# Sigmoid attention with a ReGLU layer behind it on one core: four more slices of the hidden layer as a unit of seven products, and helper work put elsewhere

## The chip, the core and the metric

The kernel runs on one core of a Trainium2 chip, with all its engines: TensorE (PE in the profile, its weight loads PEld), VectorE (DVE), ScalarE (ACT), GpSimd (POOL), SyncE (SP) and the DMA engines. The metric is the device time of one execution in microseconds (us). Three runs of the kernel before took 388.02, 388.04 and 389.07 us; their median, 388.04, is the number that the change is measured against.

## The reference, cut to what matters

```python
# q, k, v: [8 batches, 12 heads, 448 tokens, 64], fp32
scores = q @ k.T / 8 - log(448)
x = (sigmoid(scores) @ v)          # heads side by side: [3584 tokens, 768]
out = (relu(x @ w_gate) * (x @ w_val)) @ w_out   # 768 -> 1536 -> 768
```

The attention has no softmax: each score goes through a sigmoid by itself. The layer behind it multiplies a gated half with a value half.

## The kernel before, in words

**Units.** A batch has three groups g of four heads, and each group seven chunks of 64 keys. One pair (g, c) is a *qk unit* (`qk_unit`, L299): PE makes the scores of four heads in two PSUM banks, and ACT puts each bank through the sigmoid (L187) into an SBUF tile PT. When all seven chunks of a group are there, `pv_group` (L307, matmuls at L257) multiplies them with v into two banks, and DVE copies these, scaled, into the transposed x (`xT`, L184). The hidden layer is cut into twelve slices f of 128 columns. For one batch and one slice, `gv` (L311) makes a gate bank and a value bank (L322), takes the relu of the gate on ACT (L334) or on DVE (L336), and multiplies the two on DVE into `hT` (L343).

**Seven products.** Where two batches or two halves of a batch are there together, the kernel uses Strassen's scheme: a 2x2 block product with seven products instead of eight, at the price of sums of blocks on DVE before it (S from the weights, T or X from the data) and of additions behind it. `gv_split` (L698) does four slices f for the two halves of one batch, `gv_pair` (L598) two slices for two batches, `down_pair` (L452) the last product for two tiles of 128 tokens. A unit of `gv_split` is called s0 or s4 here, by its first slice; one of `down_pair` y(g, p), with g the pair of batches and p the pair of tiles. The sums over `w_out` are T1 to T4 (`weight_sums`, L399); the sums of slices for s0 and s4 are made step by step in batch 1 (`early_sum_steps`, L560).

**PSUM.** There are eight banks in a ring. `bank` (L77) gives the next one, and `later` (L85) moves banks to the ring's end. A matmul that starts in a bank waits until whoever read its last content is done; PE runs its matmuls in the order of the program, so all that follows waits too.

**The order of the work** is written out by hand (`manual_schedule`): each engine runs its instructions in the order in which the program calls them. The 21 qk units of batch b are cut into *bursts* (`cuts`, L936 and L938). Behind each burst PE does one piece of the hidden layer for batches that are already through, and while that runs, ACT works off the burst's sigmoids. In batch 1 the pieces are a queue of half units (batch 0's 256 and 192 tokens one after the other, `push_first`, L770, `ffn_mix`, L774), so many after each burst as `mix` says (L948), with PE transposes of batch 1's keys and queries hung in between (`hooks`). In batch 2 they are `work`: u8, s0, u9, s4, u10, u11 (L888), where u8 is a plain `gv` of batch 1 with slice 8. In batch 3 they are y(0,0), y(0,1) and y(0,2) for the first two batches. A `down_pair` may have a further burst in its middle (`amid`); those in `SUMS_LATE` (L407) make the next unit's sums around it.

**Keys and queries** from batch 2 on are transposed by DMA: `dma_transposes` (L218) copies ("re-lays") a group's k and q into a tile `rel`, of which there are two, and SP sends a transposing DMA into `qkT`. Loads from HBM go through POOL's queue, in order; `hold` (L866) is a tiny POOL copy that reads a `qkT` tile, so that the loads behind it start only when that transpose has landed. In the kernel before, `late_loads` (L873) in the last stretch of batch 1 puts batch 2's v, batch 3's k and q and `w_out` behind such a hold.

Of the kernel before, what the change touches and what calls it, by code (L numbers as in the profile page):

```python
# [18 lines left out]
def kernel(  # L19
# [38 lines left out]
    ysbp = ctx.enter_context(tc.tile_pool(name="ysbp", bufs=4))  # L58
    gsbp = ctx.enter_context(tc.tile_pool(name="gsbp", bufs=6))
    first_sbuf = ExitStack()  # L60
    early = first_sbuf.enter_context(tc.tile_pool(name="early", bufs=1))
# [33 lines left out]
    def tiles_of(b):  # L95
        if b not in in_tiles:
            pool = early if b == 1 else inp
# [58 lines left out]
    load(1, 1, 2, "kq")  # L156
    load_gv(6, 9)
    load_v(1)
    load(1, 2, 3, "kq")
    load_gv(9, 12)  # L160

# [55 lines left out]

    def dma_transposes(b, g):  # L218
        k16, q16, _ = in_tiles[b]
        rel = relp.tile([P, TW, P], FP16, tag="rel", name="rel")  # L220
        for ti, t16 in enumerate((k16, q16)):
            nc.vector.tensor_copy(  # L222
                rel[:, ti * NCH : (ti + 1) * NCH, :].rearrange("p c (h d) -> p h c d", h=2),
                t16[:, 2 * g : 2 * g + 2, :].rearrange("p h (c d) -> p h c d", c=NCH),
            )
        nc.sync.dma_start_transpose(
            qkT_of(b, g)[:], rel[:].rearrange("p c x -> p (c x)")
        )

    def row_of(r, hh):  # L230
# [139 lines left out]
    def open_late():  # L370
        first_sbuf.close()
        pool = ctx.enter_context(tc.tile_pool(name="late", bufs=1))
        T = pool.tile([P, 3, HF, HM], FP16, tag="T", name="T")
        late["T"] = [T[:, 0], T[:, 1], wo[:, 0:HF, HM:DM], T[:, 2]]
        late["odd"] = pool.tile([P, NFC, P], FP16, tag="odd", name="odd")
        late["X"] = pool.tile([P, 3, HD, S], FP16, tag="X", name="X")
        late["sums"] = ctx.enter_context(tc.tile_pool(name="sums", bufs=2))

    def sub(o, a, b):
# [26 lines left out]
    FRESH = {1: 0, 2: 0, 3: NPP}  # L406
    SUMS_LATE = {(1, 0), (1, 1), (2, 0), (2, 1), (3, NPP)}  # L407
    odd = {}
# [43 lines left out]
    def down_pair(g, p, beside, then, last, first_copy, amid=None):  # L452
# [106 lines left out]

    def early_sum_steps(j, f):  # L560
        views = []
        for i in range(3 * j, 3 * j + 3):
            t = early.tile([P, 2, 512], FP16, tag=f"PT{i}", name="S")
            flat = t[:].rearrange("p a y -> p (a y)")[:, 0 : HD * 2 * P]
            views.append(flat.rearrange("p (x y) -> p x y", y=2 * P))
        yield lambda: gate_sums(f, f + 2)
        yield from unit_sum_steps(("s", f), f, views)

    def unit_sum_steps(key, f, tiles):
# [3 lines left out]
        S3, A22 = wv[:, 0:HD, fs], wv[:, HD:NDC, fs]  # L573
        sums[key] = S1, S2, S4
        return (
# [5 lines left out]
    def batch_blocks(g, ks):  # L581
        x1, x2 = xT_tiles[2 * g], xT_tiles[2 * g + 1]
        lo, hi = slice(*ks), slice(HD + ks[0], HD + ks[1])
        return [late["X"][:, i, lo] for i in range(3)] + [x1[:, lo], x1[:, hi], x2[:, lo], x2[:, hi]]

# [12 lines left out]
    def gv_pair(g, f, beside, first_copy):  # L598
        x1, x2 = xT_tiles[2 * g], xT_tiles[2 * g + 1]
        T1, T2, T4 = (late["X"][:, i] for i in range(3))  # L600
        B11, B21, T3, B22 = x1[:, 0:HD], x1[:, HD:NDC], x2[:, 0:HD], x2[:, HD:NDC]
# [82 lines left out]
    def split_sums(b):  # L684
        tile_ = xTp.tile([P, NPAIR, S], FP16, tag="xT", name="X2")
        flat = tile_[:].rearrange("p a s -> p (a s)")
# [5 lines left out]
        B11, B21, B12, B22 = x[:, 0:HD, 0:SQ], x[:, HD:NDC, 0:SQ], x[:, 0:HD, SQ:S], x[:, HD:NDC, SQ:S]  # L692
        sub(T1, B12, B11)
        sub(T2, B22, T1)
        sub(T4, B21, T2)
        sub(T3, B22, B12)

    def gv_split(b, f, beside):  # L698
# [8 lines left out]
        for j in range(4):  # L707
            us, fs = slice(j % 2 * P, (j % 2 + 1) * P), slice((f + j) * P, (f + j + 1) * P)
            S1, S2, S4 = (t[:, :, us] for t in sums[("s", f + j // 2 * 2)])
            sets.append((  # L710
                wg[:, 0:HD, fs], wg[:, HD:NDC, fs], wv[:, HD:NDC, fs],
                S1, S2, wv[:, 0:HD, fs], S4,
            ))
# [136 lines left out]
    slots[5].pv()  # L850
    push_first(1, range(0, 4))
    for f0 in range(4, 12, 2):
        for half in range(2):
            for f in range(f0, f0 + 2):
                push_first(half, (f,), (half, f) not in ((0, 9), (1, 8)))

# [8 lines left out]

    def hold(b, g):  # L866
        nc.gpsimd.tensor_copy(gate[0:1, :], qkT_tiles[(b, g)][0:1, 0, 0:2])
# [12 lines left out]

    work = deque()

    pending = []

    def push_group(g):
# [22 lines left out]
    def next_work(jobs=(), alone=False, amid=None, ahead=()):  # L908
# [11 lines left out]
        if kind == "y":  # L920
            down_pair(g, i, beside, prepare, not work, scaled_act if alone else scaled, amid)
        elif amid:
# [11 lines left out]
    for b in range(1, B):  # L934
        if b == 1:
            cuts, pv_at = (0, 3, 6, 9, 13, 17, 21), {3: (0, 2), 5: (1, 2)}  # L936
        else:
            cuts, pv_at = (0, 4, 7, 11, 14, 18, 21), {0: (-1, 2), 2: (0, 2), 4: (1, 2)}  # L938
        bursts = list(range(len(cuts) - 1))
# [7 lines left out]
        if b == 1:  # L947
            mix = (4, 3, 3, 3, 3, 4)  # L948
            hooks = {
                1: [(3, lambda: both(1, 1))],  # L950
                3: [(3, lambda: both(1, 2))],
                4: [(2, lambda: dma_transposes(2, 0)), (0, lambda: dma_transposes(2, 1))],
                5: [(4, late_loads)],
            }
            steps = itertools.chain.from_iterable(early_sum_steps(j, 2 * j) for j in range(4))
            given = ((0, 0, 1, 1, 1), (0, 1, 1, 1), (0, 1, 1, 1), (0, 1, 1, 0), (2, 0, 0, 0), (0, 1, 1, 1, 0))
        else:
            mix = (0,) * count

        def burst(n):  # L960
            for i, (g, c) in enumerate(order[cuts[n] : cuts[n + 1]]):
# [9 lines left out]
                qk_unit(b, g, c)  # L971

        for m in range(count):
# [4 lines left out]
            if b == 2 and m == 3:  # L978
                jobs += [lambda: dma_transposes(3, 0), lambda: dma_transposes(3, 1)]
            elif b == 3 and m == count - 1:  # L980
                jobs.append(lambda: dma_transposes(4, 1))
# [5 lines left out]
            if b == 1:  # L987
                if m == 0:
                    load(2, 0, 1, "kq")
                    load(2, 1, 2, "kq")  # L990
                    load(2, 2, 3, "kq")
            elif m == (2 if b == 4 else 0) and b + 1 < B:
# [3 lines left out]
            if b == 2 and m == 0:  # L996
                ahead.append(lambda: split_sums(1))
            elif b == 2 and m == 4:
                open_late()
                first_sums = token_sum_steps(0, 0)  # L1000
                ahead += [*first_sums[:2], lambda: weight_sums(0)]
            elif b == 2 and m == 5:
                ahead += [lambda: weight_sums(1), lambda: dma_transposes(3, 2)]
                jobs += first_sums[2:]
            elif b == 3 and m == 0:
                jobs.append(lambda: (weight_sums(2), weight_sums(3)))
            elif b == 3:
                jobs.append(lambda: gate_sums(6 + 2 * m, 8 + 2 * m))
                if m == 1:
                    jobs.append(lambda: keep_odd(0))  # L1010
            if b % 2 and b > 2:
                if m == count - 1:
                    jobs.append(lambda: (batch_sums_t1(b // 2), batch_sums(b // 2, (0, 1))))
            elif b == 4 and m == 0:
# [51 lines left out]
```

## Time and profile before

| | |
|---|---|
| median of three runs | 388.04 us (388.02 to 389.07) |
| the profiled execution | 388.3 us, of which 386.5 us are the span from the first to the last instruction |
| mean granted TensorE clock | 0.999 |
| busy: PE, DVE, ACT, POOL | 381.1, 304.9, 227.3, 49.8 us |
| batch 1's bursts begin | 29.01 us |
| batch 2's bursts begin | 61.30 us |
| batch 3's bursts begin | 95.81 us |
| y(0,0) begins | 98.02 us |

Times on the left of a timeline row are us from the span's start, the second number is how long the row lasted. Rows merge instructions of one kind that follow each other; the bracket gives the engine's idle time before the row and what ended it. Starts of matmuls can be taken at their word, their ends are modelled and overlap with the next. So the price of a piece of PE work is read here from its start to the start of what follows.

### The profile page before, as it was taken

The numbers are of one execution on the slowest core, as the hardware profiler recorded it, in microseconds if no ns is written. First come the engines' busy times: TensorE is split into PE (matmuls) and PEld (weight loads), VectorE is DVE, ScalarE is ACT, GpSimd is POOL, SyncE is SP. The second block draws the span as 40 slices with busy tenths as digits, with TensorE's granted clock in tenths as the row PEclk, the third lists the DMA queues.
The fourth block names the chain that finished last, engine by engine and source line by source line (L and its number), as shares of the span: only waits on it lengthen the run. The fifth ranks groups of instructions, "written<-read, shape, count | busy, mean of one in ns | idle before, by whom it ended". The sixth has DMA issues, their size and how long they took to land.

```text
span 386.5 us, 8978 instructions
## 1 busy us (share of the span) xinstructions
PE 381.1 (99%) x3570; PEld 223.2 (58%) x3570; DVE 304.9 (79%) x611; ACT 227.3 (59%) x480; POOL 49.8 (13%) x73
## 2 busy tenths in 40 slices
PE   8999999999999999999999999999999999999996
PEld 6678776885555545455555554545455555555654
DVE  3455667769868999999868789999978788999653
ACT  5967887567777645455777764545477344333322
POOL 8643306100400003000300300000000000000000
PEclk9999999999999999999999999999999999999999
DMA  9999999999979302952499893222013220000235
GB/s 171 199 199 204 204 193 161 208 208 135 179 168 178 81 2 37 182 95 47 43 229 220 171 233 56 44 54 50 0 28 76 72 75 0 2 0 0 73 92 165
DMA packets 67563, 43.81 MB, mean 113 GB/s; under 512 B 35648, under 2 KB 64192, under 8 KB 67520
## 3 DMA queue, kind: packets, MB, share of 16 engines
q0 software_dynamic: 28960, 23.24, 39.2%
q1 hardware_dynamic: 37792, 19.34, 24.5%
q10 hardware_dynamic: 768, 0.66, 0.6%
q8 instruction: 28, 0.46, 0.5%
q14 instruction: 15, 0.12, 0.1%
HBM read 47.19 MB, written 11.01 MB: 151 GB/s over the span
## 4 chain that ended last, share of the span: by engine, by line
PE 96%; ACT 2%; DMA 1%; DVE 0%; issue 0%
PE u L389 34%; PE g L389 16%; PE y L389 12%; PE qk_ps L239 10%; PE pv_ps L257 8%; PE g_ps L322 5%; PE v_ps L322 5%; PE u L718 2%; PE g L718 2%; ACT PT L187 2%; DMA qkT<-rel 1%; PE warm_ps L175 1%; PE trt L204 1%; DVE ysb L544 0%; DVE zeros L130 0%
## 5 line engine op out<-in xcount | busy, mean ns | idle before, releaser
L187 ACT ACTIVATE PT<-qk_ps 128x448 f16<-128x448 f32 (+3 forms) x318 | 150.9, 584 | 79.2 <-PE qk_ps L239 79.1
L389 PEld LDWEIGHTS <-S 128*128 128x128 f16 x576 | 56.3, 98 | 45.9
L628 DVE TENSOR_TENSOR gsb<-g,gsb 128x448 f32<-128x448 f32 x72 | 42.7, 623 | 7.9 <-PE g L389 7.5
L239 PE MATMUL qk_ps<-qkT 64*64 64x448 f16 (+2 forms) x756 | 47.5, 337 | 0.7 <-DMA qkT<-rel 0.3
L389 PEld LDWEIGHTS <-hT 128*128 128x128 f16 x318 | 29.5, 98 | 24.0 <-issue 6.1
L257 PE MATMUL pv_ps<-PT,v 64*64 64x448 f16 (+2 forms) x756 | 36.6, 329 | 0.0
L468 DVE SCALAR_TENSOR_TENSOR ysb<-y,ysb 128x384 f32<-128x384 f32 x33 | 18.3, 555 | 20.7 <-PE y L389 14.1
L184 DVE TENSOR_SCALAR xT<-pv_ps 128x448 f16<-128x448 f32 (+2 forms) x53 | 27.8, 566 | 8.0 <-PE pv_ps L257 6.9
L389 PEld LDWEIGHTS <-wg 128*128 128x128 f16 x216 | 20.2, 98 | 21.8 <-issue 4.3
L389 PEld LDWEIGHTS <-wv 128*128 128x128 f16 x216 | 21.1, 98 | 19.7
L450 ACT ACTIVATE ysb<-u 128x384 f32<-128x384 f32 x28 | 13.8, 491 | 30.9 <-PE u L389 26.8
L389 PE MATMUL u<-wo,hT 128*128 128x384 f16 x156 | 29.8, 327 | 0.0
L239 PEld LDWEIGHTS <-qkT 64*64 64x64 f16 x756 | 17.6, 106 | 21.0 <-issue 14.1
L111 POOL DMA_DIRECT2D k<-in_k_dram x14 | 10.8, 775 | 141.0 <-DVE rel L222 135.9
L257 PEld LDWEIGHTS <-v 64*64 64x64 f16 x756 | 21.4, 107 | 11.1 <-issue 0.5
L389 PE MATMUL u<-xT,wg 128*128 128x448 f16 x108 | 23.5, 354 | 0.0
L389 PE MATMUL u<-xT,wv 128*128 128x448 f16 x108 | 23.4, 352 | 0.0
L389 PE MATMUL g<-X,S 128*128 128x448 f16 x108 | 23.4, 352 | 0.0
L389 PE MATMUL u<-X,S 128*128 128x448 f16 x108 | 23.4, 352 | 0.0
L389 PE MATMUL g<-xT,S 128*128 128x448 f16 x108 | 23.4, 352 | 0.0
L389 PE MATMUL g<-xT,wg 128*128 128x448 f16 x108 | 23.4, 352 | 0.0
L389 PE MATMUL u<-X,wv 128*128 128x448 f16 x108 | 23.4, 352 | 0.0
(98 smaller groups left out, 563.9 us busy)
## 6 DMA issues: line engine op xcount, KB each, us to landing
out_dram<-ysb SPq DMA_DIRECT2D x53, 192.0 KB, 3.1
v<-in_v_dram POOLq DMA_DIRECT2D x8, 336.0 KB, 15.3
v<-in_v_dram POOLq DMA_DIRECT2D x16, 168.0 KB, 15.1
k<-in_k_dram POOLq DMA_DIRECT2D x4, 672.0 KB, 11.6
q<-in_q_dram POOLq DMA_DIRECT2D x4, 672.0 KB, 14.8
wo<-in_moe_w_out_dram POOLq DMA_DIRECT2D x2, 1152.0 KB, 19.2
k<-in_k_dram POOLq DMA_DIRECT2D x9, 224.0 KB, 11.8
q<-in_q_dram POOLq DMA_DIRECT2D x7, 224.0 KB, 12.3
```

Of the source, the lines that this page charges most:

```text
L111: nc.gpsimd.dma_start(t16[:, xs, cs], rows_of(src, b)[:, xs, cs])
L175: nc.tensor.matmul(ps[:, 0:n], zeros[:, 0:P], zeros[:, 0:n], start=True, stop=True)
L184: nc.vector.tensor_scalar(out=xT, in0=src, scalar1=XSCALE, scalar2=None, op0=AOP.mult)
L187: nc.scalar.activation(PT_ap, ps_ap, AF.Sigmoid, bias=sig_bias, scale=qk_scale)
L239: nc.tensor.matmul(out_of(hh)[o : o + 64, :], qkT[rows, c, cols], qkT[rows, NCH + c0 : NCH + c1, cols], start=True, stop=True, tile_positi ...
L257: nc.tensor.matmul(ps[hh][64 * r : 64 * r + 64, 0:qn], v16[rows, 2 * g + hh, c * D : (c + 1) * D], pieces[c][rows, hh, :], start=(c == 0), ...
L322: nc.tensor.matmul(ps[:, 0:qn], (wg, wv)[i][:, dc, f * P : (f + 1) * P], xT_tiles[b][:, dc, q0 : q0 + qn], start=(dc == 0), stop=(dc == ND ...
L389: nc.tensor.matmul(ps[:, 0:n], A[:, k_, :], W[:, k_, :], start=(first and k_ == 0), stop=(k_ == kn - 1), skip_group_check=True,)
L450: nc.scalar.activation(o, ps[:, 0:HM], AF.Copy, scale=OUT_SCALE)
L468: nc.vector.scalar_tensor_tensor(out=o, in0=ps[:, 0:HM], scalar=OUT_SCALE, in1=o, op0=AOP.mult, op1=AOP.add)
L628: nc.vector.tensor_tensor(out=gs[u][i][:], in0=ps[u][:, 0:S], in1=gs[u][i][:], op=AOP.add)
L718: nc.tensor.matmul(ps[j // 2][:, j % 2 * SQ : (j % 2 + 1) * SQ], sets[j][i][:, k_, :], W[:, k_, :], start=(first and j % 2 == 0 and k_ == ...
```

## The change

Slices 8 to 11 of batch 1, four plain units before, become a third unit of seven products, s8. Its sums need space: they lie in the output tiles `ysb`, which nothing uses until y(0,0). Batch 0's slices 10 and 11 leave the queue of half units and become whole units in batch 2. Batch 1's `mix` falls from 20 half units to 16, batch 2's bursts from six to five (three of them of five units). Around that, helper work moves: re-laying copies of batch 3 from DVE to ACT, group 2 of batch 2 from the end of batch 1 into s0, the T sums from batch 2's last two units into s8 and y(0,0), loads within POOL's queue, the relu of five half units from ACT to DVE and of one the other way.

```diff
-    load_gv(6, 9)
     load_v(1)
+    load_gv(6, 9, (0,))
     load(1, 2, 3, "kq")
-    load_gv(9, 12)
+    load_gv(6, 9, (1,))
...
-    def dma_transposes(b, g):
+    def dma_transposes(b, g, copy=nc.vector.tensor_copy):
...
-    SUMS_LATE = {(1, 0), (1, 1), (2, 0), (2, 1), (3, NPP)}
+    SUMS_LATE = {(0, 0), (1, 0), (1, 1), (2, 0), (2, 1), (3, NPP)}
...
             product(a, A12, B21)
             plus(y1[:, lo], a)
+            for job in behind[:1]:
+                job()
...
             product(c, S4, B22, False)
             plus(y1[:, hi], c)
+            for job in behind[1:]:
+                job()
+            del behind[:]
...
-    push_first(1, range(0, 4))
-    for f0 in range(4, 12, 2):
+    push_first(1, range(0, 3))
+    push_first(1, (3,), False)
+    by_vector = {(1, 3), (0, 5), (0, 6), (1, 6), (1, 7), (0, 9)}
+    for f0 in range(4, 10, 2):
...
+    def loads_behind_second():
+        hold(qkT_tiles[(2, 1)])
+        load_gv(10, 12)
+        load_v(2)
+
     def late_loads():
         dma_transposes(2, 2)
-        hold(2, 1)
-        load_v(2)
-        load(3, 0, NG, "kq")
+        load(3, 0, 1, "kq")
+        load(3, 1, NG, "kq")
         load_o()
+        load_v(3)
...
-            work.extend([("u", 1, 8), ("s", 1, 0), ("u", 1, 9), ("s", 1, 4), ("u", 1, 10), ("u", 1, 11)])
+            work.extend([("s", 1, 0), ("u", 0, 10), ("s", 1, 4), ("u", 0, 11), ("s", 1, 8)])
...
-            cuts, pv_at = (0, 4, 7, 11, 14, 18, 21), {0: (-1, 2), 2: (0, 2), 4: (1, 2)}
+            cuts = (0, 5, 8, 13, 16, 21) if b == 2 else (0, 4, 7, 11, 14, 18, 21)
...
-            mix = (4, 3, 3, 3, 3, 4)
+            mix = (3, 2, 3, 2, 3, 3)
...
-            given = ((0, 0, 1, 1, 1), (0, 1, 1, 1), (0, 1, 1, 1), (0, 1, 1, 0), (2, 0, 0, 0), (0, 1, 1, 1, 0))
+            given = ((0, 0, 2, 1), (0, 1, 1), (1, 1, 1, 1), (1, 1, 1), (0, 0, 1, 1), (1, 0, 1, 0))
...
+            if b == 2:
+                if m == 0:
...
+                    ahead.append(of_tokens[1])
+                    jobs += [late_loads, of_tokens[3], of_tokens[2], *some(1)]
+                elif m == 1:
+                    ahead += some(1)
+                    jobs += some(1)
+                elif m == 2:
+                    jobs += [*some(3), lambda: dma_transposes(3, 0, nc.scalar.copy)]
+                elif m == 3:
...
+                    ahead += some(2)
+                    jobs.append(first_sums[0])
+                else:
+                    jobs += [
+                        lambda: weight_sums(0), first_sums[1],
+                        lambda: dma_transposes(3, 1, nc.scalar.copy),
+                        lambda: dma_transposes(3, 2, nc.scalar.copy),
+                    ]
+            elif b == 3 and m == 0:
+                ahead.append(lambda: weight_sums(1))
                 jobs += first_sums[2:]
-            elif b == 3 and m == 0:
-                jobs.append(lambda: (weight_sums(2), weight_sums(3)))
+                behind[:] = [lambda: weight_sums(2), lambda: weight_sums(3)]
```

`some(n)` gives n steps of the sums for slices 8 to 11. A new pool `mid` holds batch 1's keys and queries, later the token sums of the split units and those of `gv_pair`. Slices 9 and 10 to 11 of the gate and value weights are now loads of their own: slice 9 right behind slices 6 to 8, slices 10 and 11 behind the hold. y(0,0) now makes its first copy on ACT.

More of the change, by code (lines that the diff above doesn't have):

```diff
@@ L59 @@
     gsbp = ctx.enter_context(tc.tile_pool(name="gsbp", bufs=6))
+    mid = ctx.enter_context(tc.tile_pool(name="mid", bufs=1))
     first_sbuf = ExitStack()
@@ L96, in tiles_of @@
         if b not in in_tiles:
-            pool = early if b == 1 else inp
+            pool = mid if b == 1 else inp
             in_tiles[b] = tuple(
@@ L221, in dma_transposes @@
         for ti, t16 in enumerate((k16, q16)):
-            nc.vector.tensor_copy(
+            copy(
                 rel[:, ti * NCH : (ti + 1) * NCH, :].rearrange("p c (h d) -> p h c d", h=2),
@@ L228, in dma_transposes @@
         )
+        return rel
     def row_of(r, hh):
@@ L375, in open_late, with open_X @@
         late["odd"] = pool.tile([P, NFC, P], FP16, tag="odd", name="odd")
-        late["X"] = pool.tile([P, 3, HD, S], FP16, tag="X", name="X")
         late["sums"] = ctx.enter_context(tc.tile_pool(name="sums", bufs=2))
+    def open_X():
+        k16, q16 = (mid.tile([P, NPAIR, S], FP16, tag=t, name="X") for t in ("k16", "q16"))
+        late["X"] = [k16[:, 0:HD], k16[:, HD:NDC], q16[:, 0:HD]]
     def sub(o, a, b):
@@ L564, in early_sum_steps, with output_views, unit_sum_steps @@
             flat = t[:].rearrange("p a y -> p (a y)")[:, 0 : HD * 2 * P]
[L565 to L569, printed above, removed]
+            yield flat.rearrange("p (x y) -> p x y", y=2 * P)
+    def output_views():
+        for _ in range(4):
+            t = ysbp.tile([P, 2, HD, 2 * P], FP16, tag="ysb", name="S")
+            yield t[:, 0]
+            yield t[:, 1]
+    def early_sum_steps(f, views, apart=False):
+        tiles = list(itertools.islice(views, 3))
+        fs = slice(f * P, (f + 2) * P)
+        S3 = next(views) if apart else wv[:, 0:HD, fs]
+        yield lambda: sub(S3, wg[:, 0:HD, fs], wv[:, 0:HD, fs])
+        yield from unit_sum_steps(("s", f), f, tiles, S3)
+    def unit_sum_steps(key, f, tiles, S3=None):
         S1, S2, S4 = tiles
@@ L572, in unit_sum_steps @@
         A11, A12 = wg[:, 0:HD, fs], wg[:, HD:NDC, fs]
-        S3, A22 = wv[:, 0:HD, fs], wv[:, HD:NDC, fs]
-        sums[key] = S1, S2, S4
+        S3 = wv[:, 0:HD, fs] if S3 is None else S3
+        A22 = wv[:, HD:NDC, fs]
+        sums[key] = (S1, S2, S4, S3) if key[0] == "s" else (S1, S2, S4)
         return (
@@ L583, in batch_blocks @@
         lo, hi = slice(*ks), slice(HD + ks[0], HD + ks[1])
-        return [late["X"][:, i, lo] for i in range(3)] + [x1[:, lo], x1[:, hi], x2[:, lo], x2[:, hi]]
+        return [late["X"][i][:, lo] for i in range(3)] + [x1[:, lo], x1[:, hi], x2[:, lo], x2[:, hi]]
     def batch_sums_t1(g):
@@ L599, in gv_pair @@
         x1, x2 = xT_tiles[2 * g], xT_tiles[2 * g + 1]
-        T1, T2, T4 = (late["X"][:, i] for i in range(3))
+        T1, T2, T4 = late["X"]
         B11, B21, T3, B22 = x1[:, 0:HD], x1[:, HD:NDC], x2[:, 0:HD], x2[:, HD:NDC]
@@ L684, in split_sums @@
     def split_sums(b):
-        tile_ = xTp.tile([P, NPAIR, S], FP16, tag="xT", name="X2")
+        tile_ = mid.tile([P, NPAIR, S], FP16, tag="k16", name="X2")
         flat = tile_[:].rearrange("p a s -> p (a s)")
@@ L692, in split_sums @@
         B11, B21, B12, B22 = x[:, 0:HD, 0:SQ], x[:, HD:NDC, 0:SQ], x[:, 0:HD, SQ:S], x[:, HD:NDC, SQ:S]
[L693 to L696, printed above, removed]
+        return (
+            lambda: sub(T1, B12, B11),
+            lambda: sub(T2, B22, T1),
+            lambda: sub(T4, B21, T2),
+            lambda: sub(T3, B22, B12),
+        )
     def gv_split(b, f, beside):
@@ L708, in gv_split @@
             us, fs = slice(j % 2 * P, (j % 2 + 1) * P), slice((f + j) * P, (f + j + 1) * P)
-            S1, S2, S4 = (t[:, :, us] for t in sums[("s", f + j // 2 * 2)])
+            S1, S2, S4, S3 = (t[:, :, us] for t in sums[("s", f + j // 2 * 2)])
             sets.append((
                 wg[:, 0:HD, fs], wg[:, HD:NDC, fs], wv[:, HD:NDC, fs],
-                S1, S2, wv[:, 0:HD, fs], S4,
+                S1, S2, S3, S4,
             ))
@@ L850 @@
     slots[5].pv()
-    push_first(1, range(0, 4))
-    for f0 in range(4, 12, 2):
+    push_first(1, range(0, 3))
+    push_first(1, (3,), False)
+    by_vector = {(1, 3), (0, 5), (0, 6), (1, 6), (1, 7), (0, 9)}
+    for f0 in range(4, 10, 2):
         for half in range(2):
             for f in range(f0, f0 + 2):
-                push_first(half, (f,), (half, f) not in ((0, 9), (1, 8)))
+                push_first(half, (f,), (half, f) not in by_vector)
     order = [(g, c) for g in range(NG) for c in range(NCH)]
@@ L864, with hold @@
     open_banks("ring1")
-    def hold(b, g):
-        nc.gpsimd.tensor_copy(gate[0:1, :], qkT_tiles[(b, g)][0:1, 0, 0:2])
+    def hold(t):
+        nc.gpsimd.tensor_copy(gate[0:1, :], t[0:1, 0, 0:2])
     def both(b, g):
@@ L871, in both @@
         pe_transposes(b, g, 1)
+    def loads_behind_second():
+        hold(qkT_tiles[(2, 1)])
+        load_gv(10, 12)
+        load_v(2)
     def late_loads():
         dma_transposes(2, 2)
-        hold(2, 1)
-        load_v(2)
-        load(3, 0, NG, "kq")
+        load(3, 0, 1, "kq")
+        load(3, 1, NG, "kq")
         load_o()
+        load_v(3)
     work = deque()
     pending = []
+    behind = []
     def push_group(g):
@@ L920, in next_work @@
         if kind == "y":
-            down_pair(g, i, beside, prepare, not work, scaled_act if alone else scaled, amid)
+            down_pair(g, i, beside, prepare, not work, scaled_act if alone or (g, i) == (0, 0) else scaled, amid)
         elif amid:
@@ L947 @@
         if b == 1:
-            mix = (4, 3, 3, 3, 3, 4)
+            mix = (3, 2, 3, 2, 3, 3)
             hooks = {
-                1: [(3, lambda: both(1, 1))],
-                3: [(3, lambda: both(1, 2))],
+                1: [(1, lambda: both(1, 1))],
+                3: [(2, lambda: both(1, 2))],
                 4: [(2, lambda: dma_transposes(2, 0)), (0, lambda: dma_transposes(2, 1))],
-                5: [(4, late_loads)],
+                5: [(3, loads_behind_second)],
             }
-            steps = itertools.chain.from_iterable(early_sum_steps(j, 2 * j) for j in range(4))
-            given = ((0, 0, 1, 1, 1), (0, 1, 1, 1), (0, 1, 1, 1), (0, 1, 1, 0), (2, 0, 0, 0), (0, 1, 1, 1, 0))
+            steps = itertools.chain.from_iterable(early_sum_steps(2 * j, early_views(j)) for j in range(4))
+            given = ((0, 0, 2, 1), (0, 1, 1), (1, 1, 1, 1), (1, 1, 1), (0, 0, 1, 1), (1, 0, 1, 0))
         else:
@@ L971, in burst @@
                 qk_unit(b, g, c)
+        if b == 2:
+            of_tokens = split_sums(1)
+            of_tokens[0]()
         for m in range(count):
@@ L977 @@
                 jobs.append(lambda: dma_transposes(b, 2))
-            if b == 2 and m == 3:
-                jobs += [lambda: dma_transposes(3, 0), lambda: dma_transposes(3, 1)]
-            elif b == 3 and m == count - 1:
+            if b == 3 and m == count - 1:
                 jobs.append(lambda: dma_transposes(4, 1))
@@ L988 @@
                 if m == 0:
+                    load_gv(9, 10)
                     load(2, 0, 1, "kq")
@@ L991 @@
                     load(2, 2, 3, "kq")
-            elif m == (2 if b == 4 else 0) and b + 1 < B:
+            elif b > 2 and m == (2 if b == 4 else 0) and b + 1 < B:
                 for g0, g1 in ((0, 1), (1, NG)) if b == 3 else ((0, NG),) if b > 3 else ():
@@ L995 @@
                 jobs.append(lambda: load_v(b + 1))
[L996 to L1003, printed above, removed]
-                jobs += first_sums[2:]
-            elif b == 3 and m == 0:
-                jobs.append(lambda: (weight_sums(2), weight_sums(3)))
[L1007 to L1010, printed above, removed]
+            if b == 2:
+                if m == 0:
+                    views = output_views()
+                    steps = itertools.chain.from_iterable(early_sum_steps(f, views, f == 10) for f in (8, 10))
+                    some = lambda n: [lambda: next(steps)()] * n
+                    ahead.append(of_tokens[1])
[6 more added lines that the diff above has]
+                elif m == 3:
+                    open_late()
+                    first_sums = token_sum_steps(0, 0)
+                    ahead += some(2)
[8 more added lines that the diff above has]
+                ahead.append(lambda: weight_sums(1))
+                jobs += first_sums[2:]
+                behind[:] = [lambda: weight_sums(2), lambda: weight_sums(3)]
+            elif b == 3 and m == 1:
+                jobs += [lambda: keep_odd(0), lambda: gate_sums(10, 12)]
@@ L1011 @@
             if b % 2 and b > 2:
                 if m == count - 1:
+                    if b == 3:
+                        open_X()
                     jobs.append(lambda: (batch_sums_t1(b // 2), batch_sums(b // 2, (0, 1))))
```

4 lines of the change are left out of this document (2 added, 2 removed).

## The prediction

> **What bounds the kernel now.** I read the busy table first, then the chain of work that ended last, then what PE waited for.
>
> ```profile
> PE 381.1 (99%) x3570; PEld 223.2 (58%) x3570; DVE 304.9 (79%) x611; ACT 227.3 (59%) x480; POOL 49.8 (13%) x73
> ...
> PE 96%; ACT 2%; DMA 1%; DVE 0%; issue 0%
> ```
>
> The waits with PE as the waiting engine (us in total, times, longest):
>
> ```profile
> PE qk_ps L239 <- DMA qkT<-rel: 0.3, 1, 0.3
> PE qk_ps L239 <- ACT PT L187: 0.3, 1, 0.3
> ```
>
> PE is the bound and hardly ever waits: its waits after the start are two of 0.3 us. So the change can gain only the PE time that it takes out, and each new wait of PE is paid in full. I therefore price the PE work from start to start, then go through the places where the tighter order lets PE come before a bank is free. All is against the profiled execution (388.3 us, 0.26 above the median 388.04).
>
> **PE work.** Batch 2's first burst, a plain unit, a burst of three and s0:
>
> ```profile
> 61.30 0.57 PE L239 MATMUL qk_ps<-qkT 64*64 64x448 f16 x8
> 61.71 1.49 PE L257 MATMUL pv_ps<-PT,v 64*64 64x448 f16 x28
> 61.73 3.60 ACT L187 ACTIVATE PT<-qk_ps 128x448 f16<-128x448 f32 x8 [0.48 <-PE qk_ps L239]
> ...
> 63.23 1.15 DVE L184 TENSOR_SCALAR xT<-pv_ps 128x448 f16<-128x448 f32 x2 [1.40 <-PE pv_ps L257]
> 63.51 1.31 PE L322 MATMUL g_ps<-xT,wg 128*128 128x448 f16 x6
> ...
> 65.88 0.76 PE L239 MATMUL qk_ps<-qkT 64*64 64x448 f16 x12
> 66.58 1.32 PE L718 MATMUL u<-xT,wg 128*128 128x224 f16 x12
> ...
> 74.73 0.57 PE L239 MATMUL qk_ps<-qkT 64*64 64x448 f16 x8
> ```
>
> The starts give 63.51 - 61.30 = 2.21 for a burst of four with its pv, 65.88 - 63.51 = 2.37 for a plain unit, 0.70 for a burst of three, 74.73 - 66.58 = 8.15 for a unit of seven products. A fifth qk unit adds 0.19 (the same row's step from unit to unit: 2 in 0.38). A half unit takes 0.99 with 192 tokens (31.70 to 32.69, below) and 1.31 with 256 (36.69 to 38.00).
> - Batch 1 loses two half units of each kind: -(2 x 0.99 + 2 x 1.31) = -4.60.
> - Batch 2 was 3 x 2.21 + 3 x 0.70 + 4 x 2.37 + 2 x 8.15 = 34.51, just 61.30 to 95.81. It becomes 3 x 2.40 + 2 x 0.70 + 2 x 2.37 + 3 x 8.15 = 37.79: +3.28.
> - One pair of transposes of batch 1 now stands between two half units instead of right behind a burst: one more change of tile shape. Where transposes stand behind a burst now, they begin 0.29 behind its last unit (34.17 to 34.46), 0.10 more than the next unit would. Bounds 0 and 0.2; I take 0.10.
>
> Together -1.22. This is the most the change can bring, 0.31%.
>
> **Wait (a): batch 1's second burst.**
>
> ```profile
> 31.70 0.66 PE L322 MATMUL g_ps<-xT,wg 128*128 128x192 f16 x6
> ...
> 32.47 0.62 DVE L343 TENSOR_TENSOR hT<-gate_sb,v_ps 128x192 f16<-128x192 f32 x2 [2.62 <-ACT gate_sb L334]
> 33.01 0.55 DVE L380 TENSOR_TENSOR wv<-wg,wv 128x768 f16<-128x768 f16 x1
> 33.48 0.34 DVE L343 TENSOR_TENSOR hT<-gate_sb,v_ps 128x192 f16<-128x192 f32 x1
> 33.74 0.55 DVE L380 TENSOR_TENSOR S<-wv 128x768 f16<-128x768 f16 x1
> ```
>
> DVE cannot begin these products before ACT has done six sigmoids and a relu (idle 2.62). Today four half units and two transposes come before PE wants the third one's value bank again. Afterwards the first stretch has three half units: the burst starts at 32.78, the next half unit's gate at 33.47, its value product at 33.97, in the ring's bank of the third half unit. And `given` puts the S step before that product on DVE: 33.01, S at 33.60 (a dependent sum follows 0.59 behind), product 34.07 to 34.42. PE goes on about 0.05 behind a releaser (in the row 51.01, behind a sigmoid ending 50.96), so 34.47: **0.50** lost. Bounds 0 and 0.6.
>
> **Wait (b): bursts of five.** Two units, pv and three units take 5 x 2 + 2 = 12 banks of eight. The seven products then start in the pv's banks, which DVE's xT copies free: the first ends at 63.86, 2.56 behind the burst's start, so PE goes on at 2.61 instead of 2.40. (The fifth unit waits for the fourth sigmoid, at 2.33; that lies within.) Today a plain unit or y takes a bank whose sigmoid was long done. Three bursts: **0.63**, bounds 0 and 0.9.
>
> **Wait (c): T4 in y(0,0).** With `SUMS_LATE`, y(0,0) has the order of y(1,1):
>
> ```profile
> 199.91 0.56 DVE L468 SCALAR_TENSOR_TENSOR ysb<-y,ysb 128x384 f32<-128x384 f32 x1 [2.44 <-PE y L389]
> 200.38 0.55 DVE L438 TENSOR_TENSOR S<-hT 128x768 f16<-128x768 f16 x1
> ...
> 201.41 1.14 PE L389 MATMUL y<-T,hT 128*128 128x384 f16 x6
> 201.61 0.56 DVE L468 SCALAR_TENSOR_TENSOR ysb<-u,ysb 128x384 f32<-128x384 f32 x1
> 202.09 0.55 DVE L445 TENSOR_SCALAR ysb<-u 128x384 f32<-128x384 f32 x1
> ...
> 202.88 1.49 PE L257 MATMUL pv_ps<-PT,v 64*64 64x448 f16 x28
> ```
>
> The last DVE row frees the bank of the following pv's second half at 202.64; that half is due at 202.92, so 0.28 is spare. Now T4 (1.35 long, 1.26 to the next: 99.68 to 100.94) stands behind the first row. First, the product with T4, due at 201.41, waits until 200.38 + 1.35 + 0.05 = 201.78: 0.37. Then everything behind T4 is 1.26 later, the bank is free at 203.90, and pv, by then due at 203.29, waits 0.61 more: **1.0** in all. T2 and T3 fit: T3 is done 4.9 behind y(0,0)'s start, due at 5.7. Bounds 0.4 and 1.3.
>
> **What I cost at nothing, and its cover.** DVE's added work (six sums of 0.55, one more gate sum of 0.55, the additions of s8) lies in the 4.2 us between a split unit's start and its first addition (66.58 to 70.81). Its four fullest fillings there, down to T1 and a token sum in s8, end by 3.7; an overrun would delay a bank by its own length. The six re-laying copies on ACT: DVE needs 0.39 each; on ACT 768 elements take 0.81 and 1024 take 1.02, so I take 0.92 for 896, between 0.39 and 1.02. In s8 the unit's own copies end 4.25 in, four re-layings add 3.7, the next sigmoid is due at 8.58: 0.6 spare. By the Trainium skill (ScalarE: Activation LUTs, What ACT_TABLE_LOAD costs) one takes 186 + 0.833 x 896 = 932 ns, an estimate that leaves the sum as it is; its Rules for kernel authors put such copies on VectorE, which speaks against the move, and costs the span something only where the 0.6 is gone.
>
> Loads: gate and value slices 6 to 8 were landed at 34.5 and 37.4, now behind v and, for the values, batch 1's last keys and queries: 43, due at 45. Batch 2's keys come earlier (1.15 MB of weights before them became 0.38). The hold ends near 57, then 1.44 MB at 157 GB/s (4.99 MB of loads in 60.73 to 92.58) is there by 67: slice 10 is due at 68.7, and its weights are first; v is due at 71.5. `w_out`'s halves land near 83 and 90; T1 reads the first at 89, y(0,0) the second at 98.
>
> **Sum.** -1.22 + 0.50 + 0.63 + 1.00 = +0.9. 388.3 + 0.9 = 389.2 for a profiled execution, 388.9 beside the median: within 0.3% (1.16 us), about what a measurement of this kernel can tell from no change.
>
> **Rivals.**
> 1. *The waits do not come* (releases run ahead of my rows, or the order on DVE has more air): -1.2, 386.8. For it: today PE passes the same places without a wait. Against: the three releases are worked out from rows within 0.1, and PE runs in order. One or two of three missing lies in the forecast's own range, 387.9 to 389.6.
> 2. *ACT held by a re-laying copy* (slower). Group 2's copy needs the tile `rel` of group 0, whose transpose starts near 79.8, in the middle of the load queue. The slowest of six landings between 50 and 100 took 11.0, median 5.6, and the slowest is this one, issued at 82.66 and landed at 93.61, 1.0 behind the last load. Taking 11.0 it lands at 90.8, and the copy is due at 93.6. If it lands with the loads' end instead (5.76 MB from 57.5: 94.2, so 95.2), ACT's copies end at 97.0, batch 3's first sigmoids are 1.0 late and hold PE 0.9: 389.8. It decides from a landing at 94. By the Trainium skill (DMA: Bandwidth & Descriptors, Queues, rings and completion order) an engine takes queues in turn, so a transpose would not wait for the loads' end; by that rule this rival does not happen. The trace cannot tell, as both ended together.
>
> **Chances.** Forecast 0.60, rival 1 0.18, rival 2 0.22. Faster by over 0.3% is half of rival 1: 0.09. Slower: 0.18 of rival 2 and 0.12 from the forecast's upper part: 0.30. The rest, 0.61, is within. The range reaches to both rivals, 386.8 to 390.1.
>
> **What would show it.** The unit of slices 8 to 11 lasts 8.15 or so, and batch 2's first burst starts near 57.3 instead of 61.30: 4.60 less, with wait (a) and the transposes on top. (a): the value product of the fourth half unit (slice 3, 192 tokens) starts 1.0 behind its gate product instead of 0.5. (b): 2.6 from each five-unit burst's start to its unit. (c): y(0,0)'s last product starts late and pv pauses after its first two matmuls. Rival 2 shows as ACT idle in s8 before the last two re-layings. I am wrong if PE's time to y(0,0)'s start falls by over 0.8, or if PE waits for a load.

## The result and the profile after

The changed kernel takes 394.04 us (median of six runs, 392.26 to 394.71) against 388.03 for the kernel before (six runs by now): a ratio of 1.0144, 95% interval 1.0118 to 1.017. It is 1.4% slower, outside my range of 386.8 to 390.1. The profiled execution is the quickest of the six, 392.26 us with a span of 390.4, which is 3.9 more than before.

The busy row and the shares of the chain, from the page of the changed kernel:

```profile
PE 381.1 (98%) x3582; PEld 225.4 (58%) x3582; DVE 313.1 (80%) x623; ACT 230.9 (59%) x480; POOL 52.7 (13%) x77
...
PE 88%; DMA 6%; ACT 3%; DVE 2%; issue 0%; DVEq 0%; ACTq 0%
```

PE is as busy as before, to the tenth of a microsecond, but the chain is now 6% DMA and 3% ACT. PE's waits of the changed kernel (us in total, times, longest) say where:

```profile
PE qk_ps L241 <- DMA qkT<-rel: 2.8, 1, 2.8
...
PE v_ps L324 <- DVE hT L345: 0.3, 1, 0.3
PE y L394 <- DVE T L385: 0.2, 1, 0.2
PE pv_ps L259 <- DVE ysb L450: 0.2, 1, 0.2
```

The last three rows are the waits (a) and (c) of my forecast. The first is one wait of 2.8 us for a transpose. The timeline of the changed kernel, rows of PE and ACT (start, length, what ran, idle time before it and its releaser):

```profile
28.55 0.76 PE L241 MATMUL qk_ps<-qkT 64*64 64x448 f16 x12
...
33.01 0.67 PE L324 MATMUL g_ps<-xT,wg 128*128 128x192 f16 x6
34.01 0.66 PE L324 MATMUL v_ps<-xT,wv 128*128 128x192 f16 x6 [0.33 <-DVE hT L345]
...
56.83 0.57 PE L241 MATMUL qk_ps<-qkT 64*64 64x448 f16 x8
...
59.48 1.32 PE L741 MATMUL u<-xT,wg 128*128 128x224 f16 x12
...
92.18 0.94 ACT L223 COPY rel<-q 128x896 f16<-128x896 f16 x1
98.18 0.94 ACT L223 COPY rel<-k 128x896 f16<-128x896 f16 x1 [5.06 <-DMA qkT<-rel]
98.20 0.57 PE L241 MATMUL qk_ps<-qkT 64*64 64x448 f16 x8 [2.77 <-DMA qkT<-rel]
99.03 0.94 ACT L223 COPY rel<-q 128x896 f16<-128x896 f16 x1
99.86 3.57 ACT L188 ACTIVATE PT<-qk_ps 128x448 f16<-128x448 f32 x8
...
101.32 1.14 PE L394 MATMUL u<-wo,hT 128*128 128x384 f16 x6
...
108.34 1.14 PE L394 MATMUL y<-T,hT 128*128 128x384 f16 x6 [0.21 <-DVE T L385]
...
110.33 1.51 PE L259 MATMUL pv_ps<-PT,v 64*64 64x448 f16 x26 [0.17 <-DVE ysb L450]
111.50 0.72 PE L241 MATMUL qk_ps<-qkT 64*64 64x448 f16 x8
112.15 1.15 PE L394 MATMUL u<-wo,hT 128*128 128x384 f16 x6
```

and, of the kernel before, the first rows of batch 3, y(0,0) and y(0,1):

```profile
95.81 0.57 PE L239 MATMUL qk_ps<-qkT 64*64 64x448 f16 x8
...
98.02 1.15 PE L389 MATMUL u<-wo,hT 128*128 128x384 f16 x6
...
107.95 1.15 PE L389 MATMUL u<-wo,hT 128*128 128x384 f16 x6
```

s8 starts at 87.20 and takes 8.15, so PE is ready for batch 3 at 95.35. Its first burst reads the tile that the transpose (3,0) fills, and that lands at 98.16 (issued at 79.28, 18.9 us). PE starts 2.85 late. ACT waits for the same landing, because the copy for (3,2) reuses the tile of (3,0); so the sigmoids begin at 99.86, and the burst takes 98.20 to 101.32 = 3.12 instead of 2.21, another 0.91.

The profiled execution adds up from start to start. Batch 1 began 0.46 earlier (28.55 for 29.01), batches 1 and 2 together take 66.80 in both kernels, and from 95.35 on the changed kernel needs 295.05 against 290.69 from 95.81: 4.36 more. Of these 2.85 and 0.91 are this landing, and 0.90 is wait (c): from the start of y(0,0) to that of y(0,1) it is 10.83 us (101.32 to 112.15) instead of 9.93. The wait of 0.3 for a transpose that the kernel before had at 212.8 is gone. With the earlier start of batch 1 that is +3.9.

### The profile page after: what moved, and what is told of

Same layout as the page of the kernel before. It is cut to its first block, busy times and chain, and to the rows that moved or that the text cites. A ratio compares the mean times of both kernels' runs of the same rounds, so it can differ in the third digit from the quotient of the medians.

```text
span 390.4 us, 9012 instructions
## 1 busy us (share of the span) xinstructions
PE 381.1 (98%) x3582; PEld 225.4 (58%) x3582; DVE 313.1 (80%) x623; ACT 230.9 (59%) x480; POOL 52.7 (13%) x77
## 4 chain that ended last, share of the span: by engine, by line
PE 88%; DMA 6%; ACT 3%; DVE 2%; issue 0%; DVEq 0%; ACTq 0%
PE u L394 34%; PE g L394 16%; PE y L394 12%; PE qk_ps L241 8%; PE pv_ps L259 8%; DMA qkT<-rel 5%; PE g_ps L324 3%; PE v_ps L324 3%; ACT PT L188 3%; PE u L741 2%; PE g L741 1%; DMA ysb<-in_k_dram 1%; PE trt L205 1%; ACT rel L223 0%; DVE T L385 0%
## 5 line engine op out<-in xcount | busy, mean ns | idle before, releaser
L241 PE MATMUL qk_ps<-qkT 64*64 64x448 f16 (+2 forms) x756 | 48.5, 336 | 3.6 <-DMA qkT<-rel 2.8
L473 DVE SCALAR_TENSOR_TENSOR ysb<-y,ysb 128x384 f32<-128x384 f32 x34 | 18.9, 556 | 21.9 <-PE y L394 14.8
L241 PEld LDWEIGHTS <-qkT 64*64 64x64 f16 x756 | 18.6, 105 | 24.7 <-issue 15.3
```

Of the source, the lines that this page charges most:

```text
L241: nc.tensor.matmul(out_of(hh)[o : o + 64, :], qkT[rows, c, cols], qkT[rows, NCH + c0 : NCH + c1, cols], start=True, stop=True, tile_positi ...
L473: nc.vector.scalar_tensor_tensor(out=o, in0=ps[:, 0:HM], scalar=OUT_SCALE, in1=o, op0=AOP.mult, op1=AOP.add)
```

## The experiments

My theory, T, is that a transpose takes turns with the loads packet by packet, so that wide load packets beside it make it late. Its rivals are E, that a transpose lands only when all earlier loads are through (98.16 behind 97.92 in the changed kernel, 93.61 behind 92.58 before), and A, that the copies moved to ACT are the cause. Each of the runs is an edit of the changed kernel; from run 7 on, each builds on the one that it names. Line numbers can be off by a few, and an expectation may call run 9 by its label, e10_hold_third. "Profiled" is the time of the execution with the trace, the median is that of all runs, and the ratio is to runs of the kernel before that were made beside them.

**1. v of batch 3 behind the transpose**

```diff
+    def v_behind_first():
+        hold(qkT_tiles[(3, 0)])
+        load_v(3)
...
         load_o()
-        load_v(3)
...
-                    jobs += [*some(3), lambda: dma_transposes(3, 0, nc.scalar.copy)]
+                    jobs += [*some(3), lambda: dma_transposes(3, 0, nc.scalar.copy), v_behind_first]
```

> Batch 3's v is loaded behind a hold on the transpose (3,0) instead of ahead of it. Three theories of the profiled execution's 392.26 us. T (turns): a transpose has 1824 packets (1368 + 456 in the trace of before from 60 to 64 us), and beside loads each of them waits for one load packet (228 against 229 from 84 to 86 us of the changed kernel, 348 against 347 from 68 to 70). E (end of the loads): a transpose lands only once every load issued ahead of it is through (98.16 behind 97.92). A (ACT): the re-laying copies on ACT hold up the sigmoids and so PE. T: w_out ends near 92.7 with 1090 of the 1824 packets through, the rest runs alone in 1 to 1.5 us, landing 94.8, PE waits less than 0.3 us in front of batch 3. The copy of (3,2) is then 0.8 late, 0.5 us on PE. 388.5 to 389.2 in the profiled execution. E: the same within 0.5, landing 93 to 94. A: no less than 391. If PE's pause is also what lowers the granted clock (0.990 to 0.996 in four of the six runs of the changed kernel), it is 0.999 here in all runs.

Measured: 388.89 us, ratio 1.0027 (1.001 to 1.0043); profiled 389.14. (3,0) landed at 94.60, 14.6 behind its issue, and PE did not wait for it. The granted clock was 0.999 or 1.0 in all ten runs. A falls: ACT makes the same copies. T and E are not told apart.

**2. The transpose (2,2) ahead of the loads again**

```diff
     def late_loads():
-        dma_transposes(2, 2)
...
-                5: [(3, loads_behind_second)],
+                5: [(3, loads_behind_second), (1, lambda: dma_transposes(2, 2))],
```

> The transpose (2,2) goes back from s0 to the end of batch 1, ahead of the loads. T: from 66 to 78 us the loads no longer give every second packet to it (0.30 MB in 2 us become 0.41), so they end near 94.5 instead of 97.92, and from there (3,0) runs alone: it lands near 95.5, PE waits 0 to 0.5 instead of 2.9, the sigmoids are 1 late: 388.8 to 389.8 in the profiled execution. E: the same landing, one us behind the loads' end. A: 392, as ACT's copies are untouched.

Measured: 390.59 us, ratio 1.006 (1.0045 to 1.0075); profiled 390.72. The loads ended at 95.58 and (3,0) landed at 96.71, each about 1.1 later than T said; PE waited 1.1 for it, and the late sigmoids cost the burst the same 0.9 as before. So moving (2,2) into the loads made up 2.3 us of their later end, not all.

**3. The copy that waits on ACT, moved away**

```diff
                         lambda: dma_transposes(3, 1, nc.scalar.copy),
-                        lambda: dma_transposes(3, 2, nc.scalar.copy),
...
-                jobs += first_sums[2:]
+                jobs += [*first_sums[2:], lambda: dma_transposes(3, 2, nc.scalar.copy)]
```

> The re-laying of (3,2), which holds ACT 5.06 us for the tile of (3,0), goes from s8 into y(0,0). T and E: (3,0) lands as late as before, so PE waits 2.9 us all the same in front of batch 3, and only the 0.91 us go that the late sigmoids cost the first burst: 391.2 to 391.6 in the profiled execution. A: the whole 3.8 us go: 388.5. The granted clock, if PE's pause lowers it, is still below 0.998 in some runs.

Measured: 393.56 us, ratio 1.0145 (1.0121 to 1.017). PE's wait stayed (2.6), as T and E say, so A falls a second time. But the profiled execution took 393.55, some 2 us more than I expected. The windows table of this run shows why (window, its length, then busy time and instructions of PE, PEld, DVE, ACT, POOL; then the granted clock, the DMA share and GB/s):

```profile
95.00:98.50 3.50, 0.92 (x10) 0.66 (x7) 2.65 (x5) 0.00 (x0) 0.00 (x0) 0.95 1.29 138
98.50:100.00 1.50, 1.45 (x16) 0.73 (x20) 0.00 (x0) 0.82 (x2) 0.00 (x0) 0.50 0.77 174
100.00:102.00 2.00, 2.00 (x32) 0.96 (x24) 0.05 (x1) 1.03 (x3) 0.00 (x0) 0.61 0.00 0
```

After the pause PE works at half clock: 0.35 us of the first window, all of the second and 1.56 of the third, 3.4 us together. The burst takes 98.55 to 102.22, 3.67 instead of 2.21, so 1.46 of the 2 us are the clock; some 0.3 more is a wait in y(0,0) for a copy that stood behind the moved ones on ACT. Of the six runs of the changed kernel, the two with a clock of 0.999 or 1.0 have spans of 390.4 and 391.0, the four with 0.990 to 0.996 have 392.2 to 392.9. Run 6 tests this.

**4. w_out in narrower packets**

```diff
-            nc.gpsimd.dma_start(
-                wo[:, f0:f1, :], moe_w_out[f0 * P : f1 * P, :].rearrange("(c p) m -> p c m", p=P)
-            )
+            for ms in (slice(0, HM), slice(HM, DM)):
+                nc.gpsimd.dma_start(
+                    wo[:, f0:f1, ms],
+                    moe_w_out[f0 * P : f1 * P, ms].rearrange("(c p) m -> p c m", p=P),
+                )
```

> w_out is loaded in column halves: the same bytes in the same order, but packets of 768 bytes instead of 1536. T: the transpose (3,0) then passes its 1824 packets at the rate that it had beside packets of 896 bytes (347 in 2 us, not 225): 10.6 us from its first packet at 83.2, landing 94 to 95, while the loads still end near 98. PE waits less than 0.3 us: 388.5 to 389.2 in the profiled execution. E: (3,0) lands at 98 with the loads, 392.3. A: 392.3.

Measured: 388.98 us, ratio 1.0019 (1.0009 to 1.0028); profiled 389.09. (3,0) landed at 95.10, the last load at 98.93: the transpose is 3.8 ahead of the loads' end, with the same loads in the same order. E falls, T holds. The DMA tables (queue: packets, MB, share of time) of the changed kernel from 70 to 72 us, beside loads with packets of 896 bytes:

```profile
q0 software_dynamic: 348, 0.30, 90.7%
q1 hardware_dynamic: 347, 0.09, 33.0%
```

from 84 to 86 us, beside `w_out` with packets of 1536 bytes:

```profile
q0 software_dynamic: 227, 0.35, 94.3%
q1 hardware_dynamic: 227, 0.06, 21.9%
```

and of this run from 84 to 86 us, with 768 bytes:

```profile
q0 software_dynamic: 386, 0.28, 90.6%
q1 hardware_dynamic: 383, 0.10, 36.5%
```

The loads are q0, the transposes q1. In each pair the two queues move the same number of packets, to within three, whatever their size: 256 bytes of the transpose (0.09 MB by 347) against 768, 896 or 1536 of the loads (a few small packets among q0's make its mean a little less). The wider the load's packet, the slower the transpose. This is what the Trainium skill states (DMA: Bandwidth & Descriptors, Queues, rings and completion order: an engine takes its queues in turn, packet by packet), and the trace agrees by the counts above. What I read from it was wrong: taking turns does not mean that the transpose comes through soon.

**5. The transpose issued earlier**

```diff
-                    jobs += [*some(3), lambda: dma_transposes(3, 0, nc.scalar.copy)]
+                    jobs += [lambda: dma_transposes(3, 0), *some(3)]
```

> All loads as in the changed kernel; only the re-laying of (3,0) goes from ACT, behind the copies of s4, to DVE, ahead of the sums in s4, so that its transpose is issued near 75.5 us instead of 79.28 and its packets can follow those of (2,2) at 79, not at 83.2. T (a packet of the transpose for each packet of the loads): 1824 packets beside w_out at 113 in a us reach about 1500 by the end of w_out, near 93, and the rest runs beside v's smaller packets: landing near 95, 2.5 to 3 us ahead of the loads' end, which stays near 98. PE waits 0 to 0.5 us in front of batch 3: 388.6 to 389.6 in the profiled execution. E (it lands behind the loads): 98, 392.3.

Measured: 391.08 us, ratio 1.0073 (1.0057 to 1.0089); profiled 390.91. Issued at 76.16, (3,0) landed at 96.44 and the last load at 98.02. That is ahead of the loads, against E, but 1.4 later than I worked out by T, so PE still waited 0.9. By the counts, the 1,824th packet behind those of (2,2) began near 95.7: from 88 to 90 us only 159 passed, against 224 to 238 in each of the three windows before, and no run shows why. The landing came 0.7 behind that. My reading, which no run tests, is that the counts are sums over 16 engines, and the landing waits for the slowest of them. It fits that in the changed kernel some 930 packets of the next transpose, (3,1), had begun before (3,0) landed, 2.0 behind the count, and that in runs 1 and 4, where none had, it landed 0.5 behind.

**6. The pause filled**

```diff
+        if b == 3:
+            ps = bank("warm_ps")
+            for _ in range(14):
+                nc.tensor.matmul(ps[:, 0:S], wg[:, 0, 0:P], wg[:, 0, 0:S], start=True, stop=True)
+            free.rotate(1)
```

> The changed kernel with 14 matmuls of 448 columns, whose result nobody reads, between s8 and batch 3: 14 x 0.187 = 2.6 us of the pause of 2.9 are filled, the transpose lands when it did. If it is the pause that lowers the granted clock (0.50 from 98.5 to 100 us and 0.61 from 100 to 102 in the trace of the kernel with (3,2) later), all runs show 0.998 or more and the median falls from 394.0 to the 392.3 of the profiled execution, within 0.5. If the clock falls for another reason, the median stays near 394 and some runs show less than 0.997.

Measured: 392.66 us, ratio 1.0115 (1.01 to 1.0131). All four runs show a clock of 0.999 or 1.0. With 14 useless matmuls the median is 1.4 us lower than without them (the intervals of the two ratios just overlap, the clocks do not: four of six runs were at 0.990 to 0.996 without them). So it is PE's idleness that lowers the clock, which fits the 18 executions of runs 1, 2 and 5: PE waits 1.1 us or less in their traces, and the clock was 0.998 or above in all of them. The profiled execution was the slowest of the four (393.11), because its batch 1 began at 29.45, 0.9 later than in the changed kernel's.

**7. T4 ahead of the addition** (on the kernel of run 4)

```diff
-            for job in behind[:1]:
+            for job in behind:
                 job()
...
-            for job in behind[1:]:
-                job()
```

> On the kernel with narrow w_out packets (388.98, 389.09 profiled), T4 is made right behind T3 in y(0,0), in DVE's gap of 0.79 us and ahead of the addition, not behind it. By my wait (c), PE's late product with T4 (0.38) and its pause in the next pv (0.35) go: 0.7 less, 388.3. The rival, that DVE is full there and another bank is then late, gives 389.0 or more.

Measured: 388.6 us, ratio 1.0013 (1.0002 to 1.0023), 0.4 below run 4 instead of 0.7; by the medians alone the two cannot be told apart, as the intervals of their ratios overlap. The traces show the 0.4: from y(0,0)'s start to y(0,1)'s it is 10.45 us, in run 4 10.84. The late product with T4 is gone (0.38), the pause in the next pv is not (1.66 us from its start to the next unit, 1.32 in the kernel before).

**8. The sums of batch 1 behind the product** (on run 7)

```diff
-            given = ((0, 0, 2, 1), (0, 1, 1), (1, 1, 1, 1), (1, 1, 1), (0, 0, 1, 1), (1, 0, 1, 0))
+            given = ((0, 0, 0, 3), (0, 1, 1), (1, 1, 1, 1), (1, 1, 1), (0, 0, 1, 1), (1, 0, 1, 0))
```

> On the kernel with narrow w_out packets, T4 ahead as in the run before, and in batch 1's first stretch the two steps of sums stand behind the third half unit's product on DVE, not ahead of it. By my waits (a) and (c), 0.49 and 0.7 go: 1.2 less, 387.8 (half of the runs above 387.5), so 0.2 to 0.3 below the kernel before. If the sums moved in batch 1 only shift the wait to a later bank, 388.3.

Measured: 387.94 us, ratio 0.9996 (0.9986 to 1.0006): 0.66 below run 7 (the intervals of the ratios just overlap), and no wait in batch 1's first stretch: batch 1 takes 27.80 us, 0.48 less than in the changed kernel. But the profiled execution (388.45) has a new one:

```profile
116.19 0.57 PE L243 MATMUL qk_ps<-qkT 64*64 64x448 f16 x8 [0.83 <-DMA qkT<-rel]
```

The transpose (3,2), issued at 96.05 beside batch 4's loads, landed only at 116.14.

**9. Batch 4's loads held until (3,2) has landed** (on run 8)

```diff
+                if b == 3:
+                    jobs.append(lambda: hold(qkT_tiles[(3, 2)]))
                 for g0, g1 in ((0, 1), (1, NG)) if b == 3 else ((0, NG),) if b > 3 else ():
```

> The kernel of the run before (T4 ahead, sums of batch 1 behind the product, narrow w_out), and batch 4's loads held until (3,2) has landed. In that kernel's profile (388.45 us) (3,2), issued at 96.05, landed at 116.14 beside batch 4's loads and held PE for 0.99 at 116.19. T: with no load beside it, (3,2) lands within 6 us of its issue (6.58 in the kernel before), the 0.99 us go from that profile and 0.2 to 0.6 from the median of 387.94, in whose runs the wait comes and goes: 387.3 to 387.7. If the later loads of batch 4 then hold its own transposes (issued at 117.8 in that profile), 388 or more.

Measured: 388.26 us, ratio 1.0004 (0.9996 to 1.0013). (3,2) landed at 102.87, 7.0 behind its issue, and the wait is gone from the trace; its profiled execution, 387.54, is 0.9 below that of run 8. The median is above the 387.3 to 387.7 that I expected and not lower than run 8's, though; in most runs of that kernel the wait can have cost little, but only one of them has a trace.

**10. The next token sums behind the copy** (on run 9)

```diff
-                for step in steps[:2]:
+                near = 0 if (g, p) == (0, 0) else 2
+                for step in steps[:near]:
...
-            for step in steps[2:]:
+            for step in steps[near if amid else 2:]:
```

> As e10_hold_third, and in y(0,0) DVE makes the next unit's first two token sums (1.05 us) behind the last copy of the second output tile, not ahead of it. By the last part of my wait (c) that copy then frees the bank 1.05 earlier and PE's pause of 0.33 in the next pv (0.41 at 105.74, less the usual 0.09) goes: 0.3 us less than e10_hold_third, 387.0 to 387.4, 0.2 to 0.3% below the kernel before. If the sums then come late for y(0,1), no gain.

Measured: 388.51 us, ratio 1.0004 (0.9993 to 1.0016). The pause in pv is gone (9.93 us from y(0,0)'s start to y(0,1)'s, as in the kernel before, instead of 10.47 in run 9), but now y(0,1) waits, as the rival says:

```profile
109.71 1.14 PE L396 MATMUL u<-T,S 128*128 128x384 f16 x6 [0.19 <-DVE ysb L452]
```

This product starts 0.35 late, so 0.35 of the 0.53 has moved along DVE's queue and is not gone. By their ratios runs 8 to 10 cannot be told from the kernel before.

## Why the prediction was wrong

**The arithmetic held.** Batches 1 and 2 took 66.80 us against 66.80. By my sum it was -4.60 + 0.10 + 0.50 for batch 1, measured 28.28 for 32.29, -4.01; and 3.28 + 0.63 for batch 2, measured 38.52 for 34.51, +4.01. The units of seven products take 8.15 (59.48 to 67.63, 73.34 to 81.49).

**Wait (a)** was right: the value product starts at 34.01, 1.00 behind its gate product, and run 8 removed it by the order on DVE alone. **Wait (b)** was right: 2.65, 2.64 and 2.64 from the start of each five-unit burst to its unit, where I said 2.61; the first xT copy ended at 59.39 and PE went on at 59.48. **Wait (c)** was right: 0.38 at the product with T4 (1.36 us behind the product before it, usually 0.98), where I said 0.37, and 0.55 from the next burst's start to y(0,1) (109.40 to 112.15, before 105.75 to 107.95), where I said 0.61. Of the 0.55, 0.37 lies in pv and the rest in the two units behind it; run 10, in which pv does not pause, does not have that rest either. Together it is 0.90 by the starts of y(0,0) and y(0,1), where I said 1.0.

With the landing taken out, the kernel is where the forecast put it: 388.89 and 388.98 us in runs 1 and 4, forecast 388.9. That it fits to 0.1 is luck. In the trace of run 1 the kernel takes 0.6 us more than the kernel before from batch 1's start to the end, not 0.9, because the old wait of 0.3 at 212.8 is gone, which I did not forecast; the start-up, which differs by some tenths from trace to trace, can fill the gap.

**The step that failed is the landing of (3,0).** My sum has no term for it, and only rival 2 prices it. I took 11.0 us for it, the longest between 50 and 100 us before, and gave a landing with the loads' end, 95.2, as the bad case. It took 18.9 and landed at 98.16. Three things were mis-sized or missing.
- *The 11.0 was not a transpose beside loads.* The kernel before had all but three packets of its loads out by 92, so that only some 530 of that transpose's 1,824 packets went beside load packets (248 and 168 from 86 to 90 us, at most 117 from 90 to 92). A transpose that has `w_out` beside it for its whole length needs 1,824 / 227 x 2 = 16 us from its first packet on.
- *The loads end at 97.92, not 94.2.* I divided their bytes by a rate measured with few packets of transposes beside them (none from 64 to 86 us). (2,2), now among the loads, takes every second packet from 66 to 79 us, and the loads move 0.30 MB in 2 us instead of 0.41 (before, from 70 to 72). Run 2 gives 2.3 of the 3.7 us back.
- *Who waits.* I let only the copy for (3,2) wait, and through ACT the sigmoids: 0.9, measured 0.91. But batch 3's first burst reads (3,0) itself, and is due at 95.35. Before, it was due at 95.81 and the tile was there at 93.61; those 2.2 us of slack I did not list among what I cost at nothing.

So the place was among my rivals, with a chance of 0.22, but not the mechanism: rival 2 has the transpose land with the loads' end, which run 4 refutes, and I counted the taking of turns as a reason against it, where it is what makes the transpose late. Its price was 0.9 where it was 3.8 in the profiled execution. The clock added the rest: the median lies 1.8 above that execution. That a pause of PE costs more than its length was in none of my cases.

What stays open: why landings come 0.5 to 2 us behind what the packet counts give and why some windows pass fewer packets (run 5), and what part of the scatter of 1 us and more in runs 7 to 10 is the start-up; batch 1 began between 28.55 and 29.45 in the traces of this case.

## What to carry to other kernels

When PE is the bound, list every transfer that PE reads with its landing and its due time, and price a change of the load queue by these slacks; a PE sum that is right to 0.1 us says nothing about them. Price a transfer beside others by packets, not by bytes or by its length in another place: here a transpose of 1,824 small packets lets as many packets of the other queue pass while that queue has work. Wide packets of a load that is in no hurry (run 4) or the place of one load (run 1) can decide more than the work that was moved.

## What the runs showed of the hardware

Where a pause of PE of 2.6 to 2.9 us stood in the program, 8 of 10 runs had a mean clock of 0.990 to 0.996 (four of six of the changed kernel, all four of run 3). The one trace among them, that of run 3 at 0.996, has about 3.4 us at half clock behind the pause; a mean of 0.990 or 0.991, as three runs had, comes to some 7 to 8 us at half clock, an estimate from the means. When matmuls filled the pause (run 6), and at pauses of about 1 us (runs 2 and 5), the clock stayed at 0.998 or above. The Trainium skill (TensorE: Matmul & The Clock Gate, What's actually happening) has the clock halved after one idle window of about 3.4 us. The length of the slow time in run 3 agrees with such a window; the idle time does not, since PE stopped at 95.85 there and the clock fell near 98.15, 2.3 us later.
